# Opening loads written out, k products by rows, a shorter last product, and one product less per batch in a fused attention and MLP kernel

## The chip, the core and the metric

One core of a Trainium2 chip runs the whole program. The metric is the device time of one execution in microseconds (us). TensorE (PE) multiplies matrices and loads its weights in parallel (PEld); VectorE (DVE), ScalarE (ACT) and GpSimd (POOL) work elementwise; SyncE (SP) only issues DMA transfers here. Each engine takes its own instructions strictly in the order in which the program lists them.

## The reference, cut to what matters

```python
# attention: 4 batches, 8 heads, 576 positions, 64 wide; masks keep a window of 32 (4 heads) or 32 with stride 4
scores = where(mask, scale * q @ k.T, -1e9);  attn = softmax(scores);  x = attn @ v        # -> (4, 576, 512)
# first MLP, on x mixed with the x of the position before
xk = mu_k * x + (1 - mu_k) * x_prev;          xr = mu_r * x + (1 - mu_r) * x_prev
y  = sigmoid(xr @ w_r) * (relu(xk @ w_k)**2 @ w_v)          # w_r 512x512, w_k 512x1024, w_v 1024x512
# second MLP: mix over positions by a rank of 32, then over channels
u   = y + (y.T @ U @ V).T                                    # U 576x32, V 32x576
out = u + relu(u @ w_ch1) @ w_ch2                            # w_ch1 512x2048, w_ch2 2048x512
```

The weights come as 64-bit floats, read as two 32-bit words; the kernel turns them into 32-bit floats on the chip.

## The kernel before, in words

**Arithmetic.** A weight piece is 128x512. To convert one (`cv_bits`, lines 385 to 392) takes an `Abs` on ACT (L385) and four DVE operations (L386, L387, L389, L392). The first MLP's 20 pieces are `w1raw`: pieces 0 to 3 are w_r, 4 to 11 w_k, 12 to 19 w_v (`places`, line 1146). The first half batch (c = 0, 288 positions) multiplies whole 32-bit floats. For c = 1 to 7 each operand is cut into a high and a low part (`hi_lo`; in the rows `wh` and `wl`, L352 on ACT and L349 on DVE or POOL), and each product becomes three faster ones (L815 to L817). `split_weight` cuts the 20 pieces while c = 1 runs; meanwhile `cv_w2` converts the second MLP's 32 pieces (tile `w`, not `wx`) and writes them to a buffer in HBM, `w2f`.

**Stages.** Attention goes by units of one head pair and one part of a batch: the first four alone (`attend`), all later ones two at a time (`attend2`). A unit's chain crosses all engines: scores on PE (L597 or L676), mask and minimum on DVE (L537), exponentials on ACT (L546), sum and reciprocal on DVE (L551, L552), scaling on POOL (L557), transposes on PE (L628 or L714), a copy on ACT (`pts`, L352), the product with v on PE (L640 or L732), a copy to `x`. `mix` makes xk and xr of it: a difference `d` on POOL, then L769 on DVE. A half batch has 20 quanta (`quanta`): 4 tiles r, 8 tiles k, 8 (for c = 0, 16 half) tiles v. For c = 0 the r products go by rows (`r_row`, L828): as soon as piece p and mix p are there, four products into four PSUM banks `psM`. Its k tiles (L812) each need four pieces at once. Then come y @ U (`y_tr`, `u_mm`, L908 to L927), @ V (`v_mm`, `us`), and the second MLP in five groups (`ch1`, `ch2`), the last lines of which add and store the result.

**Order.** The code lists operations with durations; `plan` orders them per engine, by the longest way to the end, within a window of 160 operations, and keeps the best of 24 passes. Where it sees PE idle for over 600 ns it puts in products of zeros (`zero`, L1308). So a change of the list can move instructions anywhere.

**Lines touched.** The first loads stand at lines 1176 to 1183; `single`, `visit` and `fresh` bring in the attention units; `VISIT0`, `VISIT`, `CONV0`, `SPLIT` say at which quantum a visit, a conversion or a cut is listed. The rows of U past 576 are zeros, so in the last 64 positions of a batch `u_mm` multiplies half empty tiles, which L916 clears:

```python
            nc.tensor.matmul(acc(), lhsT=us[:n, t, :], rhs=hi()[:n], start=(t == 0), stop=False)
            nc.tensor.matmul(acc(), lhsT=us[:n, t, :], rhs=lo()[:n], start=False, stop=(t == NT - 1))
```

Of the kernel before, what the change touches and what calls it, by code (L numbers as in the profile page):

```python
# [62 lines left out]
SPLIT = (-4, -4, -3, -3, -1, -1, 0, 0, 1, 1, 2, 2, 5, 5, 6, 6, 7, 7, 8, 8)  # L63
# [15 lines left out]
def tile_attention_mix_channel(  # L79
# [708 lines left out]
    def quanta(c):  # L788
# [94 lines left out]
        q += [lambda o=o: k_tile(o) for o in range(8)]  # L883
# [18 lines left out]
    def y_tr(b, t, tag):  # L902
# [10 lines left out]
        sub("DVE", DM, lambda: lo()[:n], lambda: pt()[:n], lambda: f32(hi()[:n]), [(pt,), (hi,)], [(lo,)], psum=True)  # L913
        if n < P:
            for x in (hi, lo):
                op("POOL", 250, lambda x=x: nc.gpsimd.memset(f32(x()[n:]), 0.0), [], [(x, "rest")], 40)  # L916
        yhl[b, t] = (hi, lo, P)

    def u_mm(b, t, tag):
# [3 lines left out]
        hi, lo, n = yhl.pop((b, t))  # L923
# [5 lines left out]
        pe(2 * 233, run, [(hi,), (lo,), (hi, "rest"), (lo, "rest")] + [("us", g) for g in range(4)], [(acc,)], "f32r", 400)  # L929
# [168 lines left out]
    accs = {}  # L1098

    def ch2(g, j, hid):  # L1100
# [4 lines left out]
        for o in range(4):  # L1105
            acc = accs[g][o]

            def run(o=o, acc=acc):
                a = acc()[:, :n]
                for e in range(2):  # L1110
                    wh, wl = (t()[:, o * P : (o + 1) * P] for t in rows2_w[2 * j + e])
                    xh, xl = (t()[:, e * n : (e + 1) * n] for t in (hh, hl))
                    nc.tensor.matmul(a, lhsT=wh, rhs=xh, start=(j == 0 and e == 0), stop=False)  # L1113
                    nc.tensor.matmul(a, lhsT=wl, rhs=xh, start=False, stop=False)  # L1114
                    nc.tensor.matmul(a, lhsT=wh, rhs=xl, start=False, stop=(j == 7 and e == 1))  # L1115

            pe(6 * (MMW if g else MMQ), run, [(t,) for e in range(2) for t in rows2_w[2 * j + e]] + kh, [(acc,)], "f32r")
# [3 lines left out]
        for o in range(4):  # L1121
# [8 lines left out]
            step = Q if last and o == 3 else n  # L1130
            for c0 in range(0, n, step):
                c = slice(c0, c0 + step)
                dve(step, lambda acc=acc, ot=ot, u_=u_, c=c: nc.vector.tensor_tensor(
                    out=ot()[:, c], in0=acc()[:, c], in1=u_()[:, c], op=ALU.add),
                    [(acc,), ku], [(ot, c0) if last else (ot,)], two=True, psum=True)
                dma(P * step * 4, lambda o=o, ot=ot, c=c: nc.sync.dma_start(
# [35 lines left out]
    def next_piece():  # L1172
        src, k, _ = jobs[len(loaded)]
        loaded.append(cv_load(src, k))

    a_load(0, ["qk"])
    load(P * 4 * (P + NALL * KW), lambda: nc.sync.dma_start(cst_t, cst), ("cst",))
    next_piece()
    a_load(0, ["v"])
    load(P * 32, lambda: nc.sync.dma_start(mu_t, mu), ("mu",))  # L1180
    a_load(1, ["qk"])
    next_piece()
    a_load(1, ["v"])
# [47 lines left out]
    for c in range(NCH - 1):  # L1231
        cur = quanta(c) if c else first
        for n in range(NQ):
            if c == 0:
# [168 lines left out]
```

## Time and profile before

| what | value |
|---|---|
| median of 3 runs | 758.99 us (758.56 to 760.91) |
| profiled execution, its own time | 759.92 us |
| its span, first to last instruction | 758.1 us |
| PE busy | 739.3 us, 98% |
| DVE, ACT, POOL busy | 567.9, 393.1, 388.3 us |
| mean granted clock of TensorE | 0.997 |

The profiled execution is 0.93 us above the median of the runs; 1.8 us of it lie outside the span. Busy PE includes the products of zeros, so it is not useful work alone.

### The profile page before, as it was taken

The page shows a single profiled execution, that of the slowest core. Times are in us where ns is not written, and L with a number is a line of the kernel's source. Part 1 is how long each engine was busy: PE and PEld are TensorE (multiplying, and loading weights), DVE is VectorE, ACT ScalarE, POOL GpSimd, SP SyncE. Part 2 cuts the span into 40 slices and gives each one's busy share as a digit, 9 for nine tenths or more (in the row PEclk, how much of TensorE's full clock was granted, in tenths as well). Part 3 has the DMA queues.
Part 4 walks back from the last instruction along what each step waited for, and adds up shares of the span by engine and source line. Part 5 has one row for each costly group of instructions (what it writes and reads, how often), then busy time and mean ns, then how long its engine had stood idle before and what let it go on. Part 6 is the DMA issues. An engine that isn't in the chain of part 4 may idle for free.

```text
span 758.1 us, 18341 instructions
## 1 busy us (share of the span) xinstructions
PE 739.3 (98%) x6921; PEld 677.6 (89%) x6921; DVE 567.9 (75%) x1335; ACT 393.1 (52%) x995; POOL 388.3 (51%) x408
## 2 busy tenths in 40 slices
PE   8899999999999999999999999999999999999997
PEld 6667999999999999999999998888988989898986
DVE  5999989999898845775677778675888765575632
ACT  4578795767585746372555454343453434343310
POOL 1331464646464635273765677544677554456500
PEclk9999999999999999999999999999999999999999
DMA  9767346776756540557543252132532212042001
GB/s 333 238 255 246 133 148 192 267 248 202 267 179 205 176 157 1 196 160 225 178 153 100 94 181 100 57 125 83 171 102 84 85 56 84 29 140 70 15 1 55
DMA packets 53223, 109.77 MB, mean 145 GB/s; under 512 B 5648, under 2 KB 15888, under 8 KB 53136
## 3 DMA queue, kind: packets, MB, share of 16 engines
q1 hardware_dynamic: 53136, 108.62, 43.4%
q8 instruction: 54, 0.88, 0.5%
q14 instruction: 33, 0.27, 0.1%
HBM read 86.05 MB, written 22.54 MB: 143 GB/s over the span
## 4 chain that ended last, share of the span: by engine, by line
PE 83%; DVE 7%; POOL 3%; issue 3%; DMA 3%; ACT 1%; SPq 0%; DVEq 0%; POOLq 0%; ACTq 0%
PE psM L815 10%; PE psM L816 9%; PE psM L817 9%; PE psS L1115 8%; PE psS L1113 8%; PE psS L1114 8%; PE psM L1036 7%; PE psM L1037 6%; PE psM L1038 6%; PE psM L812 4%; PE psS L732 2%; PE psS L676 1%; DMA uf<-us 1%; POOL cl L347 1%; DVE ok L1073 1%
## 5 line engine op out<-in xcount | busy, mean ns | idle before, releaser
L347 POOL TENSOR_TENSOR cl<-sums,ch 128x512 fp32r<-128x512 f32 x72 | 98.6, 1369 | 93.5 <-ACT ch L352 62.4
L1113 PE MATMUL psS<-hh,rh 128*128 128x512 f32 (+1 forms) x320 | 119.3, 373 | 1.8 <-DVE us L949 1.5
L1115 PE MATMUL psS<-hl,rh 128*128 128x512 f32 (+1 forms) x320 | 119.4, 373 | 0.4 <-DVE hl L1051 0.3
L1114 PE MATMUL psS<-hh,rl 128*128 128x512 f32 (+1 forms) x320 | 118.9, 372 | 0.0
L352 ACT ACTIVATE ch<-sums 128x512 fp32r<-128x512 f32 (+1 forms) x104 | 57.5, 562 | 104.7 <-DVE sums L472 97.0
L815 PE MATMUL psM<-xk,wh 128*128 128x288 f32 x336 | 101.7, 303 | 0.0
L816 PE MATMUL psM<-xk,wl 128*128 128x288 f32 x336 | 99.5, 296 | 0.0
L817 PE MATMUL psM<-xk,wh 128*128 128x288 f32 x336 | 99.3, 295 | 0.0
L347 POOL TENSOR_TENSOR cl<-st,ch 128x256 fp32r<-128x256 f32 x80 | 66.9, 852 | 50.9 <-PE psM L1038 34.7
L472 DVE TENSOR_TENSOR sums<-st 128x256 f32<-128x256 f32 (+1 forms) x144 | 86.2, 646 | 7.8 <-POOL cl L347 3.9
L347 POOL TENSOR_TENSOR xk<-m,xk 128x288 fp32r<-128x288 f32 x56 | 54.8, 992 | 36.2 <-ACT xk L352 18.8
L1115 PEld LDWEIGHTS psS<-hl,rh 128*128 128x128 f32 x320 | 60.3, 188 | 12.3 <-DVE hl L1093 1.0
L1113 PEld LDWEIGHTS psS<-hh,rh 128*128 128x128 f32 x320 | 60.3, 188 | 11.7 <-DVE us L949 1.7
L1114 PEld LDWEIGHTS psS<-hh,rl 128*128 128x128 f32 x320 | 60.3, 188 | 9.4
L815 PE MATMUL psM<-k2s,wh 128*128 128x288 f32 x224 | 67.2, 300 | 0.0
L816 PE MATMUL psM<-k2s,wl 128*128 128x288 f32 x224 | 66.1, 295 | 0.2 <-issue 0.2
L817 PE MATMUL psM<-k2s,wh 128*128 128x288 f32 x224 | 66.0, 295 | 0.0
L815 PEld LDWEIGHTS psM<-xk,wh 128*128 128x128 f32 x336 | 63.5, 189 | 0.7 <-DVE wl L349 0.2
L347 POOL TENSOR_TENSOR k2s<-k,k2s 128x288 fp32r<-128x288 f32 x49 | 45.1, 926 | 36.7 <-ACT k2s L352 34.2
L816 PEld LDWEIGHTS psM<-xk,wl 128*128 128x128 f32 x336 | 63.7, 190 | 0.1
L817 PEld LDWEIGHTS psM<-xk,wh 128*128 128x128 f32 x336 | 63.7, 190 | 0.0
L1093 DVE SCALAR_TENSOR_TENSOR hl<-ort,hh 128x512 fp32r<-128x512 f32 x32 | 26.0, 811 | 46.3 <-ACT hh L1092 46.2
(152 smaller groups left out, 2137.1 us busy)
## 6 DMA issues: line engine op xcount, KB each, us to landing
st<-w2f SPq DMA_DIRECT2D x96, 256.0 KB, 3.1
w<-w2raw SPq DMA_DIRECT2D x32, 512.0 KB, 5.1
w<-w1raw SPq DMA_DIRECT2D x20, 512.0 KB, 5.7
w2f<-w SPq DMA_DIRECT2D x32, 256.0 KB, 2.6
raw<-qk SPq DMA_DIRECT2D x16, 320.0 KB, 6.4
ytmp<-y SPq DMA_DIRECT2D x32, 144.0 KB, 2.6
yb<-ytmp SPq DMA_DIRECT2D x4, 1152.0 KB, 6.8
uf<-us SPq DMA_DIRECT2D x32, 144.0 KB, 1.9
```

What stands on the lines that cost most here:

```text
L347: op("POOL", t, lambda: nc.gpsimd.tensor_tensor(out=out_(), in0=a(), in1=b(), op=ALU.subtract), r, w, 40, lock=True)
L352: act(n, lambda: nc.scalar.activation(out_(), in_(), AF.Copy), r, w, psum, strided)
L472: dve(k * Q, lambda: nc.vector.tensor_tensor(out=q(sm_, n, k)(), in0=a(), in1=b(), op=op_), [(s1,), (s2,)], [(sm_, key)], two=True)
L815: nc.tensor.matmul(a, lhsT=wh, rhs=xh, start=start, stop=False)
L816: nc.tensor.matmul(a, lhsT=wl, rhs=xh, start=False, stop=False)
L817: nc.tensor.matmul(a, lhsT=wh, rhs=xl, start=False, stop=stop)
L1036: nc.tensor.matmul(a, lhsT=wh()[:, wi], rhs=xh()[:, ci], start=(k == 0), stop=False)
L1037: nc.tensor.matmul(a, lhsT=wl()[:, wi], rhs=xh()[:, ci], start=False, stop=False)
L1038: nc.tensor.matmul(a, lhsT=wh()[:, wi], rhs=xl()[:, ci], start=False, stop=(k == len(parts) - 1))
L1113: nc.tensor.matmul(a, lhsT=wh, rhs=xh, start=(j == 0 and e == 0), stop=False)
L1114: nc.tensor.matmul(a, lhsT=wl, rhs=xh, start=False, stop=False)
L1115: nc.tensor.matmul(a, lhsT=wh, rhs=xl, start=False, stop=(j == 7 and e == 1))
```

## The change

1. The first loads follow a written order (`LOADS`, `begin`, `fetch`): the second unit's q and k come before the first unit's v; one piece is converted per step in the opening (`convert_to(t + 1, 1)`).
2. For c = 0 the first four k tiles go by rows (`k_row`), as the r tiles did.
3. The first two-unit step is a `visit` at quantum 0 instead of part of the last `single`; VISIT, MIX for c = 0 and one entry of SPLIT move.
4. `plan` takes the differences `d` 20 us earlier in its ranking, and puts in fewer and partly narrower products of zeros (35 of 512 and 17 of 224 columns for 55 of 512).
5. In a batch's last 64 positions the low part goes to rows 64 to 127 of the same tile, and U is repeated there: one product instead of two, and no clearing.
6. In the last `ch2`, tile 3 is multiplied in two parts of 384 and 128 columns; its adds and stores follow the parts.

```diff
+MIX0 = ((7, 0, "r"), (8, 1, "r"), (13, 0, "k"), (13, 2, "r"), (14, 1, "k"), (17, 2, "k"), (18, 3, "r"), (19, 3, "k"))
-VISIT0 = (4, 12)
-VISIT = (1, 10)
-CONV0 = [min(20, 7 + n) for n in range(20)]
+VISIT0 = (0, 4, 12)
+VISIT = (0, 11)
+CONV0 = 7
+LOADS = ("q0 c w q1 m", "q2 v0 v1 w", "q3 v2 w w", "w w w v3", "")
-SPLIT = (-4, -4, -3, -3, -1, -1, 0, 0, 1, 1, 2, 2, 5, 5, 6, 6, 7, 7, 8, 8)
+SPLIT = (-4, -4, -3, -3, -1, -1, 0, 0, 1, 1, 2, 4, 5, 5, 6, 6, 7, 7, 8, 8)
-FILL, FILL_FROM, FILL_NS = 0.7, 600.0, 0.453
+FILL, FILL_FROM, FILL_NS, FILL_COLD = 0.6, 600.0, 0.453, 7000.0
+EARLIER = {"d": -20}
...
-            return late
+            return [late[o.i] + 1000.0 * EARLIER.get(o.kind, 0) for o in ops]
...
-                    o.before = (x, wide, int(FILL * room / (FILL_NS * wide)))
+                    pace = FILL_NS * (2 if o.at < FILL_COLD else 1)
+                    o.before = (x, wide, int(FILL * room / (pace * wide)))
...
+        def k_row(p):
+
+            if p == 0:
+                kacc.update((o, bank("M")) for o in range(4))
+            for o in range(4):
+                pe(MM1, lambda o=o: nc.tensor.matmul(
+                    kacc[o]()[:, :HS], lhsT=whole_w[2 + p, 0]()[:, o * P : (o + 1) * P], rhs=cols(xk0, 4 + p),
+                    start=(p == 0), stop=(p == 3)), [(whole_w[2 + p, 0],), (xk0, 4 + p)], [(kacc[o],)], mode, spare=True)
+            if p == 3:
+                for o in range(4):
+                    k_out(o, kacc[o])
...
-        sub("DVE", DM, lambda: lo()[:n], lambda: pt()[:n], lambda: f32(hi()[:n]), [(pt,), (hi,)], [(lo,)], psum=True)
-        if n < P:
-            for x in (hi, lo):
-                op("POOL", 250, lambda x=x: nc.gpsimd.memset(f32(x()[n:]), 0.0), [], [(x, "rest")], 40)
-        yhl[b, t] = (hi, lo, P)
+        to, rows = (lo, slice(0, n)) if n == P else (hi, slice(n, P))
+        sub("DVE", DM, lambda: to()[rows], lambda: pt()[:n], lambda: f32(hi()[:n]), [(pt,), (hi,)], [(to, "lo")], psum=True)
+        yhl[b, t] = (hi, lo) if n == P else (hi,)
...
-            nc.tensor.matmul(acc(), lhsT=us[:n, t, :], rhs=hi()[:n], start=(t == 0), stop=False)
-            nc.tensor.matmul(acc(), lhsT=us[:n, t, :], rhs=lo()[:n], start=False, stop=(t == NT - 1))
+            for i, y in enumerate(parts):
+                nc.tensor.matmul(acc(), lhsT=us[:, t, :], rhs=y(), start=(t == 0 and i == 0), stop=(t == NT - 1))
...
+    ENDS = ((0, 3 * Q // 2), (3 * Q // 2, 2 * Q))
...
+        end = g == len(GROUPS) - 1 and j == 7
+        for o, (c0, c1) in [(o, c) for o in range(4) for c in (ENDS if end and o == 3 else ((0, n),))]:
...
-            step = Q if last and o == 3 else n
-            for c0 in range(0, n, step):
+            for c0, c1 in ENDS if last and o == 3 else ((0, n),):
...
-        for u in us_:
-            if u + 2 < NU:
-                a_load(u + 2)
+        for d in (0, 2):
+            for what in ("qk", "v"):
+                for u in us_ if d == 0 or nunit > NPAIR else ():
+                    fetch(u + d, what)
...
-        single(1 if t < NPAIR else 2)
-        convert_to(t + 1)
+        begin(LOADS[t])
+        single(1 if t < NPAIR else 0)
+        convert_to(t + 1, 1)
...
-    up[:S] = um
+    up[:S], up[S:] = um, um[S - NT * P :]
```

**Place one: the first transfers and the first conversion.** SP's first eleven issues before (`raw<-qk` and `raw<-v` are a unit's operands, `w_...` the pieces; line numbers of the two kernels differ):

```order
L526 DMA raw<-qk 128x640
L1177 DMA cst_t<-cst 128x448
L368 DMA w_100<-w1raw 128x512
L530 DMA raw<-v 128x640
L1180 DMA mu_t<-mu 128x8
L526 DMA raw<-qk 128x640
L368 DMA w_106<-w1raw 128x512
L530 DMA raw<-v 128x640
L526 DMA raw<-qk 128x640
L530 DMA raw<-v 128x640
L368 DMA w_143<-w1raw 128x512
```

The same of the change:

```order
L535 DMA raw<-qk 128x640
L1208 DMA cst_t<-cst 128x448
L377 DMA w_100<-w1raw 128x512
L535 DMA raw<-qk 128x640
L1210 DMA mu_t<-mu 128x8
L539 DMA raw<-v 128x640
L535 DMA raw<-qk 128x640
L539 DMA raw<-v 128x640
L377 DMA w_135<-w1raw 128x512
L535 DMA raw<-qk 128x640
L539 DMA raw<-v 128x640
```

The second unit's scores operand moved from the sixth place to the fourth, the second weight piece from the seventh to the ninth. DVE before, behind the first unit's minimum:

```order
L551 TENSOR_SCALAR sm<-sm 128x5
L552 RECIPROCAL sm<-sm 128x5
L386 TENSOR_SCALAR wx<-wx 128x512
L387 TENSOR_SCALAR wx<-wx 128x512
L537 ISA pr,mn<-psS,cst_t 128x64
```

DVE of the change, from the same place (the lines left out are the rest of the second unit's mask and minimum):

```order
L560 TENSOR_SCALAR sm<-sm 128x5
L561 RECIPROCAL sm<-sm 128x5
L546 ISA pr,mn<-psS,cst_t 128x64
...
L395 TENSOR_SCALAR wx<-wx 128x512
L396 TENSOR_SCALAR wx<-wx 128x512
L398 SCALAR_TENSOR_TENSOR wx<-w_100,wx 128x512
L401 SCALAR_TENSOR_TENSOR wx<-w_100,wx 128x512
```

The second unit now stands ahead of the first piece's conversion.

**Place two: PE around the k tiles of c = 0.** Before (L828 is `r_row`, L812 the k tiles):

```order
L1308 MATMUL psS<-zero 128x512 x11
L714 MATMUL psS<-cst_t,pr 128x128 x4
L828 MATMUL psM<-xk_301,wx 128x288 x4
L732 MATMUL psS<-pts,raw 64x32 x32
L676 MATMUL psS<-raw 32x64 x32
L828 MATMUL psM<-xk_301,wx 128x288 x4
L812 MATMUL psM<-xk_301,wx 128x288 x20
L714 MATMUL psS<-cst_t,pr 128x128 x4
```

PE of the change (L837 is `r_row`, L852 `k_row`, L821 the k tiles that stay):

```order
L837 MATMUL psM<-xk_325,wx 128x288 x4
L852 MATMUL psM<-xk_325,wx 128x288
L723 MATMUL psS<-cst_t,pr 128x128 x4
L852 MATMUL psM<-xk_325,wx 128x288 x2
L741 MATMUL psS<-pts,raw 64x32 x32
L685 MATMUL psS<-raw 32x64 x32
L852 MATMUL psM<-xk_325,wx 128x288 x13
L1340 MATMUL psM<-zero 128x512 x3
L821 MATMUL psM<-xk_325,wx 128x288 x16
```

The last r row now stands ahead of the first pair's transposes and products with v, and 16 k products stand around these.

**Place three: DVE at the k tiles of c = 1.** Before (`w_...` on the left are pieces of the second MLP, `k_...` the k tiles' results, `wl` the cut of the first MLP's pieces):

```order
L389 SCALAR_TENSOR_TENSOR w_1065<-w_1029,w_1065 128x512
L862 SCALAR_TENSOR_TENSOR k_1369<-psM,rt 128x288
L392 SCALAR_TENSOR_TENSOR w_1065<-w_1029,w_1065 128x512
L862 SCALAR_TENSOR_TENSOR k_1369<-psM,rt 128x288
L386 TENSOR_SCALAR w_1188<-w_1188 128x512
L349 TENSOR_TENSOR wl<-wx,wh 128x512
L862 SCALAR_TENSOR_TENSOR k_1369<-psM,rt 128x288
L387 TENSOR_SCALAR w_1188<-w_1188 128x512
L349 TENSOR_TENSOR wl<-wx,wh 128x512
L862 SCALAR_TENSOR_TENSOR k_1369<-psM,rt 128x288
```

The change at the same tiles:

```order
L886 SCALAR_TENSOR_TENSOR k_1367<-psM,rt 128x288
L358 TENSOR_TENSOR wl<-wx,wh 128x512
L886 SCALAR_TENSOR_TENSOR k_1367<-psM,rt 128x288
L358 TENSOR_TENSOR wl<-wx,wh 128x512
L395 TENSOR_SCALAR w_1051<-w_1051 128x512
L886 SCALAR_TENSOR_TENSOR k_1367<-psM,rt 128x288
L358 TENSOR_TENSOR wl<-wx,wh 128x512
L886 SCALAR_TENSOR_TENSOR k_1367<-psM,rt 128x288
```

Most of the second MLP's conversions now come after these tiles.

## Rows read from the trace of the kernel before

**Rows 1.** The page: busy us, share of the span, instructions of each engine.

```profile
PE 739.3 (98%) x6921; PEld 677.6 (89%) x6921; DVE 567.9 (75%) x1335; ACT 393.1 (52%) x995; POOL 388.3 (51%) x408
```

**Rows 2.** Busy time by stretch: length, then PE, PEld, DVE, ACT, POOL, clock, DMA.

```profile
5.00:24.65 19.65, 17.51 (x327) 12.87 (x325) 15.82 (x73) 11.05 (x45) 5.75 (x8) 1.00 0.90 324
24.65:72.40 47.75, 42.88 (x531) 32.82 (x528) 46.52 (x141) 34.14 (x101) 12.40 (x16) 1.00 0.75 253
82.73:107.74 25.01, 23.61 (x295) 23.12 (x294) 23.66 (x80) 19.78 (x68) 11.75 (x15) 0.93 0.49 156
107.74:300.00 192.26, 192.10 (x2631) 188.51 (x2630) 158.64 (x467) 128.94 (x375) 104.64 (x126) 1.00 0.57 189
300.00:400.00 100.00, 97.08 (x758) 94.75 (x757) 69.98 (x115) 48.30 (x97) 57.23 (x53) 1.00 0.54 174
```

**Rows 3.** Timeline of the opening, PE and DVE: start, us, engine, line, operation.

```profile
1.46 4.10 PE L1308 MATMUL psS<-zero 128*128 128x512 f32 x9 [1.46 <-DVE zero L1304]
5.49 0.66 PE L597 MATMUL psS<-raw 64*32 64x64 f32 x40
6.17 0.23 DVE L537 CUSTOM_DVE_ANT_0 pr<-psS,cst_t 128x64 f32<-128x64 f32 x1 [4.76 <-PE psS L597]
23.96 0.69 DVE L392 SCALAR_TENSOR_TENSOR wx<-w,wx 128x512 int32<-128x512 int32 x1
41.83 2.21 PE L828 MATMUL psM<-xk,wx 128*128 128x288 f32 x8
71.09 1.29 DVE L392 SCALAR_TENSOR_TENSOR wx<-w,wx 128x512 int32<-128x512 int32 x2
```

**Rows 4.** Timeline of PE after the k tiles of c = 1.

```profile
99.42 1.37 PE L732 MATMUL psS<-pts,raw 64*64 64x32 f32 x80 [1.40 <-ACT pts L352]
101.71 0.61 PE L815 MATMUL psM<-xk,wh 128*128 128x288 f32 x1
104.28 0.30 PE L816 MATMUL psM<-xk,wl 128*128 128x288 f32 x1
104.42 0.29 PE L817 MATMUL psM<-xk,wh 128*128 128x288 f32 x1
```

**Rows 5.** First transfers: SP's issues of cst and v; us to landing.

```profile
1.19 0.42 SPq L1177 DMA_DIRECT2D cst_t<-cst  x1
2.13 0.43 SPq L530 DMA_DIRECT2D raw<-v  x1
cst_t<-cst SPq DMA_DIRECT2D x1, 224.0 KB, 3.4
raw<-v SPq DMA_DIRECT2D x1, 320.0 KB, 5.9
```

**Rows 6.** DVE's groups from 5 to 72.4 us: busy us, mean ns.

```profile
L392 DVE SCALAR_TENSOR_TENSOR wx<-w,wx 128x512 int32<-128x512 int32 x20 | 15.6, 783 | 0.2
L769 DVE SCALAR_TENSOR_TENSOR m<-d,mu_t,x 128x288 f32<-128x288 f32 x3 | 1.5, 506 | 0.0
```

**Rows 7.** Busy time by stretch around that wait, columns as above.

```profile
102.00:104.00 2.00, 2.00 (x9) 2.00 (x9) 2.00 (x18) 2.00 (x7) 1.79 (x3) 0.50 0.76 236
```

**Rows 8.** Timeline of PE at y @ U.

```profile
299.67 0.40 PE L927 MATMUL psS<-yl,us 128*128 128x512 f32 x1
299.91 0.30 PE L815 MATMUL psM<-k2s,wh 128*128 128x288 f32 x1
304.14 0.50 PE L927 MATMUL psS<-yl,us 128*128 128x512 f32 x1 [0.65 <-POOL yl L916]
```

**Rows 9.** Timeline: products of 256 columns, the last product, the last adds.

```profile
735.28 0.28 PE L1037 MATMUL psM<-tA,ch 128*128 128x256 f32 x1
735.40 0.28 PE L1038 MATMUL psM<-tA,ch 128*128 128x256 f32 x1
753.52 0.39 PE L1115 MATMUL psS<-hl,rh 128*128 128x512 f32 x1
753.95 0.76 DVE L1133 TENSOR_TENSOR ot<-psS,ug 128x256 f32<-128x256 f32 x2 [0.70 <-PE psS L1115]
```

More of the change, by code (lines that the diff above doesn't have):

```diff
@@ L62 @@
 SIDE_AT = 9
-SPLIT = (-4, -4, -3, -3, -1, -1, 0, 0, 1, 1, 2, 2, 5, 5, 6, 6, 7, 7, 8, 8)
+AHEAD = 3
+PREP = (0, 5, 12)
+SPLIT = (-4, -4, -3, -3, -1, -1, 0, 0, 1, 1, 2, 4, 5, 5, 6, 6, 7, 7, 8, 8)
 SPLIT_ENG = ("DVE",)
@@ L134, in plan @@
             o.i, o.deps, o.tiles, o.done = i, set(), [], None
+            first = o.w[0][0]
+            o.kind = first.args[2] if isinstance(first, Lazy) else first
             for k in o.r:
@@ L882, in quanta @@
         q = [lambda o=o: (r_row if whole else r_tile)(o) for o in range(4)]
-        q += [lambda o=o: k_tile(o) for o in range(8)]
+        q += [lambda o=o: (k_row if whole and o < 4 else k_tile)(o) for o in range(8)]
         if whole:
@@ L922, in u_mm @@
         acc = uacc[b]
-        hi, lo, n = yhl.pop((b, t))
+        parts = yhl.pop((b, t))
         def run():
-            nc.tensor.matmul(acc(), lhsT=us[:n, t, :], rhs=hi()[:n], start=(t == 0), stop=False)
-            nc.tensor.matmul(acc(), lhsT=us[:n, t, :], rhs=lo()[:n], start=False, stop=(t == NT - 1))
-        pe(2 * 233, run, [(hi,), (lo,), (hi, "rest"), (lo, "rest")] + [("us", g) for g in range(4)], [(acc,)], "f32r", 400)
+            for i, y in enumerate(parts):
+                nc.tensor.matmul(acc(), lhsT=us[:, t, :], rhs=y(), start=(t == 0 and i == 0), stop=(t == NT - 1))
+        pe(len(parts) * 233, run, [(parts[0],), (parts[-1], "lo")] + [("us", g) for g in range(4)], [(acc,)], "f32r", 400)
         if t == NT - 1:
@@ L1104, in ch2, with run @@
             accs[g] = [bank("S") for _ in range(4)]
-        for o in range(4):
+        end = g == len(GROUPS) - 1 and j == 7
+        for o, (c0, c1) in [(o, c) for o in range(4) for c in (ENDS if end and o == 3 else ((0, n),))]:
             acc = accs[g][o]
-            def run(o=o, acc=acc):
-                a = acc()[:, :n]
+            def run(o=o, acc=acc, c0=c0, c1=c1):
+                a = acc()[:, c0:c1]
                 for e in range(2):
                     wh, wl = (t()[:, o * P : (o + 1) * P] for t in rows2_w[2 * j + e])
[L1112 to L1117, printed above, removed]
+                    xh, xl = (t()[:, e * n + c0 : e * n + c1] for t in (hh, hl))
+                    nc.tensor.matmul(a, lhsT=wh, rhs=xh, start=(j == 0 and e == 0), stop=False, skip_group_check=c0 > 0)
+                    nc.tensor.matmul(a, lhsT=wl, rhs=xh, start=False, stop=False, skip_group_check=c0 > 0)
+                    nc.tensor.matmul(a, lhsT=wh, rhs=xl, start=False, stop=(j == 7 and e == 1), skip_group_check=c0 > 0)
+            k_acc = [(acc, c0)] if end and o == 3 else [(acc, x) for x, _ in ENDS] if g == len(GROUPS) - 1 and o == 3 else [(acc,)]
+            pe(6 * (3 + 0.4487 * (c1 - c0)), run, [(t,) for e in range(2) for t in rows2_w[2 * j + e]] + kh, k_acc, "f32r")
         if j < 7:
@@ L1129, in ch2 @@
                 u_, ku = ot, (ot,)
[L1130 to L1133 removed]
+            for c0, c1 in ENDS if last and o == 3 else ((0, n),):
+                c = slice(c0, c1)
+                dve(c1 - c0, lambda acc=acc, ot=ot, u_=u_, c=c: nc.vector.tensor_tensor(
                     out=ot()[:, c], in0=acc()[:, c], in1=u_()[:, c], op=ALU.add),
[L1135 to L1136 removed]
+                    [(acc, c0) if last and o == 3 else (acc,), ku], [(ot, c0) if last else (ot,)], two=True, psum=True)
+                dma(P * (c1 - c0) * 4, lambda o=o, ot=ot, c=c: nc.sync.dma_start(
                     out[o, :, t0 + c.start : t0 + c.stop], ot()[:, c]), [(ot, c0) if last else (ot,)], [("out", g, o, c0)])
@@ L1160, in tile_attention_mix_channel, with convert_to @@
     converted = 0
-    AHEAD = 3
-    def convert_to(n):
+    def convert_to(n, ahead=None):
         nonlocal converted
         while converted < min(n, len(jobs)):
-            while len(loaded) < min(converted + AHEAD, len(jobs)):
+            while len(loaded) < min(converted + (ahead or AHEAD), len(jobs)):
                 src, k, _ = jobs[len(loaded)]
@@ L1170, in convert_to, with fetch, begin @@
             converted += 1
[L1172 to L1183, printed above, removed]
+    fetched = set()
+    def fetch(u, what):
+        if u < NU and (u, what) not in fetched:
+            fetched.add((u, what))
+            a_load(u, [what])
+    def begin(names):
+        for x in names.split():
+            if x == "w":
+                src, k, _ = jobs[len(loaded)]
+                loaded.append(cv_load(src, k))
+            elif x == "c":
+                load(P * 4 * (P + NALL * KW), lambda: nc.sync.dma_start(cst_t, cst), ("cst",))
+            elif x == "m":
+                load(P * 32, lambda: nc.sync.dma_start(mu_t, mu), ("mu",))
+            else:
+                fetch(int(x[1:]), {"q": "qk", "v": "v"}[x[0]])
     nunit = 0
@@ L1246, in tile_attention_mix_channel @@
                 divided += 1
-            for when, p, which in MIX:
+            for when, p, which in MIX0 if c == 0 else MIX:
                 if when == n + 1:
```

10 lines of the change are left out of this document (6 added, 4 removed).

## The prediction

> **What bounds the kernel now.** The page first: PE is busy 98% of the span [rows 1], so time can only go where PE waits, runs slowly or multiplies more than it must. The stretches come next. From 107.74 to 300 us PE is busy 192.10 of 192.26 us [rows 2]: there only fewer products help. Before that it is another picture. From 24.65 to 72.40 us DVE is busy 46.52 of 47.75 us while PE, its products of zeros included, has 42.88 [rows 2]; up to 24.65 us DVE has 15.82 of 19.65 us. The timeline says what DVE makes: the fourth weight piece is ready at 23.96 + 0.69 = 24.65 us, the twentieth at 71.09 + 1.29 = 72.38 us [rows 3]. The second half of the v products of c = 0 needs pieces 16 to 19, so these 16 products cannot begin before DVE has made the last. Up to about 72 us, then, the kernel is as fast as DVE's queue, and what PE does earlier in between is worth nothing by itself. From 82.73 to 107.74 us both are near full, DVE with 23.66 of 25.01 us [rows 2], and there PE has its one long wait: 1.40 us at 99.42 us for ACT's copy of `pts`, and behind it slow products [rows 4].
>
> **The opening (parts 1 to 4).** Three things move on DVE's queue.
>
> Its start. Nine products of zeros hold PE from 1.46 to 5.56 us, so the first scores run at 5.49 and DVE begins at 6.17, 0.68 us later [rows 3]. With four instead of nine they end by about 3.3 us; the masks land at 1.19 + 3.4 = 4.59 us [rows 5], and the scores' operand stands ahead of them on the queue. DVE can begin at about 5.0 us: 1.17 us earlier.
>
> The second unit. It now stands ahead of the first piece, so whatever delays it delays the whole queue. Its operand takes the place on the transfer queue where the first v stood, which landed at 2.13 + 5.9 = 8.03 us [rows 5]. Scores at about 8.25 put its DVE work at 8.25 + 0.68 = 8.9 us. DVE has nothing else between the first unit's reciprocal, at about 7.4, and then: 1.5 us idle, beside the 1.0 us that it waits for the exponentials. Before, DVE was busy 15.82 us between 5.00 and 24.65, thus idle 1.17 + 2.66. So the idle time behind the start is about the same, and the fourth piece is ready at 24.65 - 1.17 = 23.5 us. By the queue's list, what follows up to the twentieth piece is the same work with one mix of c = 1 more, 0.51 us [rows 6]. Term **a**: 0.51 - 1.17 = -0.7 us for the twentieth piece and all behind it. Bounds: if the pieces of the new order land late or the unit ahead stalls, the start's whole gain is lost and the mix paid, +0.5; if DVE also loses its stretching, -3.0 (see the third rival).
>
> The k rows. The last r row ran at 41.83 us [rows 3]. In the new order DVE has, between the fourth piece and the mix for that row, three and a half pieces at some 2.3 us, five mixes, a pair's minima (1.3) and a reciprocal (0.4): 23.5 + 8.0 + 2.5 + 1.7 = 35.7 us. The row's four products take 2 us, the 16 k products 7.8, the pair among them 2.5, and ACT must first free the banks: PE is through by about 49. Four more pieces, a pair's minima and three mixes bring DVE to piece 11 by about 51: PE waits 2.3 us, works through four k tiles, a pair and the first v half (7.8 + 2.5 + 7.8) to 69.1, and waits 2.6 for the twentieth piece. These 4.9 us of slack are where the k rows' gain goes: nothing in the sum.
>
> **c = 1.** The wait at 99.42 us is the end of a chain: `pts` stood on ACT behind a `rt` that waits for DVE to free a slot with its k operation, and DVE had seven operations on second-MLP pieces between its first cuts for c = 1 and the fifth k result, by the order. In the new order there are two, so five fewer at 0.4 to 0.8 us, and per k tile DVE has one k and one cut, about 1.1 us where PE needs 1.7 (12 products, 0.14 apart [rows 4]). In the 192 us behind, the same sequence of transposes, copy and products passes without such a wait [rows 2]. I take the wait as gone, -1.40. [...] Ten products take 104.28 - 101.71 = 2.57 us [rows 4] in place of 1.4: 1.2 us, and they go with the wait. Term **b**: -2.6 us. Bounds: 0 (another wait of the same kind) and -2.6.
>
> **One product less (part 5).** Four batches lose one product of 512 columns each, 299.91 - 299.67 = 0.24 us apiece [rows 8], in stretches where PE has no slack. Term **c**: -0.95 us, and only a stall could hide it. At 304.14 us one of these products waited 0.65 us for POOL's clearing of the tile [rows 8], which goes; now the product waits for DVE's subtraction into the same tile, as all others do. Term **d**: -0.65 (bounds -1.0 and 0).
>
> **The end (part 6).** Before, the last product ends at 753.52 + 0.39 = 753.91 us and the two adds at 754.71 [rows 9]. Now six products of 384 and six of 128 columns replace six of 512. Products of 256 columns stand 0.12 apart [rows 9], those of 512 0.24; 384 lies at 0.18, six make 1.08. For 128 the trace has no row: at least half of 0.12, at most 0.12, the shortest spacing seen with full weights. I take 0.12, the nearest row: 1.08 + 0.72 - 1.44 = +0.36 us for the last product. The add of 384 runs beside the last six; the add of 128, about 0.3 us, ends at 753.91 + 0.36 + 0.1 + 0.3 = 754.67. Term **e**: -0.1 (bounds -0.45 with 0.06 apart, and +0.2).
> [...]
>
> **Elsewhere.** The planner reorders stretches between 300 and 740 us as well, PE waiting 2.92 us from 300 to 400 [rows 2], 0.65 of them counted above. I leave the rest at 0, within 1.5 either way.
>
> **Sum:** -0.7 - 2.6 - 0.95 - 0.65 - 0.1 = -5.0 us. Against the profiled execution's own 759.92 that is 754.9; it lies 0.93 above the median of the runs, so the median becomes **754.0 us**.
>
> **Rivals.**
> *The wait in c = 1 comes back elsewhere.* The visits moved too, and the copy of `pts` still stands behind a `rt`, now of the seventh k tile. For it: DVE's and ACT's queues are as full as before. Against it: the five operations that left. Term b falls away: 754.0 + 2.6 = 756.6 us.
> *DVE is not as tight as I think.* In the opening L392 takes 783 ns on average [rows 6] and 0.69 at most other places [rows 3]; such stretches, 20 pieces times four operations, hold some 5 us, and they fall when POOL works at the same time. The earlier `d` could free 3 of them: 754.0 - 3 = 751.0 us. Against it: POOL's work is the same.
> *Slower: PE goes cold in the opening.* There are fewer and narrower products of zeros, and with small products alone the clock has been seen to fall [rows 7]. At half clock the 32 products of r and k rows, 0.49 each, would take 15.6 us more. PE has 4.9 us of slack, so from ten such products on they cost time, and beyond 12 us of extra (25 products: the slack, the 5.0 and the 2.3 of 0.3%) the kernel is slower than before. If all run so: 754.0 + 15.6 - 4.9 = 764.7 us. Against it: at the rows PE is continuously at work, and at 104.28 it had regained its pace after ten products [rows 4].
> [...]
>
> **How the numbers follow.** Forecast 0.50, the wait elsewhere 0.30, a looser DVE 0.12, cold 0.06, others 0.02. A measurement of this kernel tells about 0.3%, 2.3 us, from no change: below 756.7 counts as faster. The forecast with its bounds (a, d, e and elsewhere, 752.5 to 757) lies there nine times in ten, 0.45; the first rival, 755 to 758.5, about four in ten, 0.13; the looser DVE always, 0.12: faster 0.70. Slower is the cold opening and a little else, 0.07; the same is what remains, 0.23. The range from 751.0 to 758.5 us leaves out the cold opening, about half of the looser DVE and the end of the first rival, some 0.15.
>
> **What would show it.** DVE's first operation at about 5.0 us; the fourth piece at 23.5, the twentieth near 71.7; c = 1 on PE about 0.7 us earlier (counting the pair that now stands behind its first tiles); no wait of PE over 0.5 us and no clock under 1.0 between 80 and 110 us; 16 products y @ U fewer by four and no clearing on POOL; the last add 0.1 to 0.4 us nearer to the start of the last products. The prediction is wrong if the twentieth piece comes later than 72.4, if PE waits anew at a copy of `pts`, if the clock falls in the opening for longer than PE's slack, or if the reordered stretches past 300 us wait 2 us more.

## The result, and the profile after

The change takes 750.62 us (median of 4, 750.15 to 751.39) where the kernel before took 759.83 beside it: ratio 0.9885, 95% interval 0.9867 to 0.9902. It is 9.2 us faster by the medians, 8.7 by the ratio; the forecast was 5.0 us. 750.62 lies 0.4 us below the lower end of the forecast's range, 751.0. The profiled execution's own time is 750.69 us, its span 748.8.

The page, as [rows 1], and busy time by stretch, as [rows 2], with one stretch more:

```profile
PE 733.4 (98%) x6920; PEld 675.5 (90%) x6920; DVE 564.4 (75%) x1335; ACT 393.1 (53%) x995; POOL 381.5 (51%) x400
```

```profile
5.00:24.65 19.65, 17.07 (x282) 13.09 (x282) 14.77 (x71) 13.41 (x52) 5.78 (x9) 0.91 0.89 312
24.65:72.40 47.75, 43.44 (x538) 33.07 (x536) 46.27 (x141) 33.71 (x102) 12.22 (x17) 1.00 0.79 268
82.73:107.74 25.01, 23.11 (x436) 22.54 (x437) 22.96 (x72) 20.28 (x65) 13.78 (x16) 0.95 0.23 75
107.74:300.00 192.26, 191.67 (x2625) 188.15 (x2624) 156.41 (x477) 128.88 (x383) 100.61 (x123) 1.00 0.60 199
300.00:400.00 100.00, 100.00 (x808) 99.22 (x807) 72.16 (x128) 51.45 (x106) 57.13 (x55) 1.00 0.56 184
105.00:108.40 3.40, 3.40 (x78) 3.23 (x75) 3.22 (x21) 3.40 (x15) 2.52 (x3) 0.51 0.66 190
```

The opening and c = 1 are no fuller than before; in the first stretch the clock is 0.91, since it stood at half from 9.5 to 12.9 us. The change is from 300 to 400 us: PE is busy all 100.00 us with 808 products, where [rows 2] had 97.08 us and 758. The timeline of PE and DVE at the places of [rows 3], [rows 4] and [rows 9], and DVE at 356 us:

```profile
3.75 0.90 PE L606 MATMUL psS<-raw 64*32 64x64 f32 x40 [0.23 <-DMA raw<-qk]
8.67 0.66 PE L606 MATMUL psS<-raw 64*32 64x64 f32 x40 [2.46 <-DMA raw<-qk]
...
4.69 0.23 DVE L546 CUSTOM_DVE_ANT_0 pr<-psS,cst_t 128x64 f32<-128x64 f32 x1 [3.29 <-PE psS L606]
...
9.35 0.23 DVE L546 CUSTOM_DVE_ANT_0 pr<-psS,cst_t 128x64 f32<-128x64 f32 x1 [2.20 <-PE psS L606]
...
15.18 0.23 DVE L546 CUSTOM_DVE_ANT_0 pr<-psS,cst_t 128x64 f32<-128x64 f32 x1 [1.13 <-PE psS L606]
...
22.91 1.28 DVE L401 SCALAR_TENSOR_TENSOR wx<-w,wx 128x512 int32<-128x512 int32 x2
...
71.61 0.68 DVE L401 SCALAR_TENSOR_TENSOR wx<-w,wx 128x512 int32<-128x512 int32 x1
...
72.44 6.54 PE L821 MATMUL psM<-k,wx 128*128 128x288 f32 x26 [0.93 <-DVE wx L401]
...
103.65 1.37 PE L741 MATMUL psS<-pts,raw 64*64 64x32 f32 x80 [1.90 <-ACT pts L361]
...
106.42 0.44 PE L825 MATMUL psM<-k2s,wl 128*128 128x288 f32 x1
106.66 0.44 PE L826 MATMUL psM<-k2s,wh 128*128 128x288 f32 x1
...
356.75 1.29 DVE L1040 TENSOR_TENSOR tmp<-ug 128x512 f32<-128x512 f32 x2 [0.38 <-DMA ug<-uf]
357.96 0.45 DVE L971 TENSOR_TENSOR us<-psS,yb 128x288 f32<-128x288 f32 x1
...
744.15 0.34 PE L1139 MATMUL psS<-hl,rh 128*128 128x384 f32 x1
...
744.72 0.27 PE L1138 MATMUL psS<-hh,rl 128*128 128x128 f32 x1
...
744.83 0.28 PE L1139 MATMUL psS<-hl,rh 128*128 128x128 f32 x1
...
745.14 0.76 DVE L1157 TENSOR_TENSOR ot<-psS,ug 128x384 f32<-128x384 f32 x2 [0.96 <-PE psS L1139]
```

The fourth piece is ready at 24.19 us, the twentieth at 72.29 (before 24.65 and 72.38, forecast 23.5 and 71.7). In c = 1 PE waits again for the copy of `pts`, longer than in [rows 4], and again runs slowly behind it (clock 0.51 from 105.0 to 108.4 us). Who made PE wait from 107.74 us to the end, before (the six longest of nine) and then after (us in total, times, longest):

```profile
PE psS L1113 <- DVE us L949: 1.5, 1, 1.5
PE psM L944 <- DVE ok L1073: 0.8, 2, 0.4
PE psS L927 <- POOL yl L916: 0.7, 1, 0.7
PE psM L1036 <- DVE ok L1073: 0.3, 1, 0.3
PE psS L1115 <- DVE hl L1051: 0.3, 1, 0.3
PE psS L927 <- DVE yl L349: 0.2, 1, 0.2
```

```profile
PE psS L685 <- issue: 0.6, 1, 0.6
PE psS L1137 <- ACT hh L1114: 0.4, 2, 0.2
PE psM L966 <- DVE ok L1095: 0.2, 1, 0.2
```

**Where the time went.** To compare kernels whose orders differ, I counted each PE product of the trace at its usual spacing (288 columns 0.1325 us, whole floats 0.2425, 512 columns 0.2325, 256 0.117, 384 0.173, 128 0.109, a score 0.013, a product with v 0.0163, zeros nothing). A transpose is entered with 0.07, too little: in fours they start 0.109 apart in both traces, and with 0.109 the bold column would be 2.2 us lower before and 2.3 in the change, the difference still -8.3. Lost time is the time at which so much useful work is done, minus that work. The columns below are cut at equal useful work (60, 80, 260, 520 and 690 us of it); the times in the head are those of the kernel before. The losses are those of one profiled execution each, which lies up to 2.5 us from the median beside it.

| lost, us | to 90.5 | to 113.7 | to 299.2 | to 571.1 | to 743.5 | median, us |
|---|---|---|---|---|---|---|
| before | 30.5 | 3.2 | 5.4 | **11.9** | 2.4 | 759.8 |
| change | 29.5 | 3.7 | 5.8 | **3.6** | 2.7 | 750.6 |
| one_product | 34.1 | 0.4 | 8.4 | **4.5** | 2.4 | 755.1 |
| one_product_shifted | 32.3 | 0.4 | 7.2 | **4.3** | 2.4 | 751.7 |
| change_shifted | 34.7 | 0.4 | 8.0 | **3.4** | 2.7 | 756.6 |
| change_realigned | 30.7 | 2.3 | 6.2 | **5.0** | 2.7 | 751.9 |
| change_realigned_warm | 29.5 | 2.3 | 6.5 | **3.8** | 2.7 | 750.6 |
| change_k_tiles | 30.9 | 0.4 | 13.4 | **3.7** | 2.7 | 756.4 |
| one_product_old_order | 31.8 | 3.4 | 5.5 | 9.6 | 2.4 | 755.8 |
| two_products | 30.6 | 0.5 | 7.6 | 9.6 | 2.7 | 759.2 |
| opening_alone | 32.6 | 0.4 | 6.3 | 8.8 | 2.7 | 757.0 |
| replan_slack | 30.1 | 0.4 | 7.6 | 8.2 | 2.3 | 757.5 |
| replan_rate | 29.9 | 2.4 | 8.8 | 8.2 | 2.7 | 758.5 |
| no_clearing | 31.8 | 0.4 | 16.0 | 9.1 | 2.7 | 763.8 |

Change against before, from the unrounded losses: -1.1, +0.5, +0.4, -8.3, +0.3 us. With four products fewer (-0.93), the six products in two parts (+0.30) and 0.44 us less between the last product and the span's end, that is -9.2. The time came from 299 to 571 us, a stretch for which the forecast had no term but the 0.65 us of the clearing (and the four products, counted apart here). In no profile does the clock fall or a wait named "issue" (see below) of over 0.4 us lie in the bold column; both occur in the first three, which makes these less sure.

### The profile page after: what moved, and what is told of

Its sections match the earlier page's. It is cut to its first block, busy times and chain, and to the rows that moved or that the text cites. A ratio compares the mean times of both kernels' runs of the same rounds, so it can differ in the third digit from the quotient of the medians.

```text
span 748.8 us, 18318 instructions
## 1 busy us (share of the span) xinstructions
PE 733.4 (98%) x6920; PEld 675.5 (90%) x6920; DVE 564.4 (75%) x1335; ACT 393.1 (53%) x995; POOL 381.5 (51%) x400
## 4 chain that ended last, share of the span: by engine, by line
PE 88%; DVE 5%; DMA 3%; ACT 2%; issue 1%; SPq 0%; POOL 0%; DVEq 0%; ACTq 0%; POOLq 0%
PE psM L824 10%; PE psM L826 10%; PE psM L825 10%; PE psS L1139 9%; PE psS L1137 9%; PE psS L1138 9%; PE psM L1058 8%; PE psM L1060 8%; PE psM L1059 8%; PE psS L741 2%; DMA w<-w1raw 2%; PE psM L821 1%; PE psS L685 1%; DVE wx L401 1%; DVE wx L398 1%; DMA raw<-qk 1%
## 5 line engine op out<-in xcount | busy, mean ns | idle before, releaser
L1137 PE MATMUL psS<-hh,rh 128*128 128x512 f32 (+2 forms) x322 | 119.5, 371 | 0.4 <-ACT hh L1114 0.4
L1139 PE MATMUL psS<-hl,rh 128*128 128x512 f32 (+2 forms) x322 | 119.6, 371 | 0.0
L1138 PE MATMUL psS<-hh,rl 128*128 128x512 f32 (+2 forms) x322 | 119.2, 370 | 0.0
L824 PE MATMUL psM<-xk,wh 128*128 128x288 f32 x336 | 100.9, 300 | 0.0
L356 POOL TENSOR_TENSOR xk<-m,xk 128x288 fp32r<-128x288 f32 x56 | 52.4, 946 | 41.2 <-ACT xk L361 33.9
L1095 DVE TENSOR_TENSOR ok<-ok,psM 128x256 f32<-128x256 f32 (+1 forms) x96 | 46.4, 504 | 22.4 <-PE psM L1060 20.0
L356 POOL TENSOR_TENSOR k2s<-k,k2s 128x288 fp32r<-128x288 f32 x49 | 43.0, 879 | 35.0 <-ACT k2s L361 32.5
```

The source lines that it names most:

```text
L356: op("POOL", t, lambda: nc.gpsimd.tensor_tensor(out=out_(), in0=a(), in1=b(), op=ALU.subtract), r, w, 40, lock=True)
L824: nc.tensor.matmul(a, lhsT=wh, rhs=xh, start=start, stop=False)
```

## The experiments

Theories: **A**, part 5 leads the planner to another order of 300 to 520 us, and that order has no waits; **B**, part 5 is worth its products and their waits, and the rest comes from other parts; **C** came up on the way: PE waits where its instructions arrive in blocks. The median of the kernel before was 758.7 us beside the first four runs, 758.8 beside the shifted and replanned ones, 759.3 beside the last four. Differences in us are differences of ratios times 759 us, those to the change by its 0.9885.

**one_product**: part 5's lines in the kernel before.

```diff
-            nc.tensor.matmul(acc(), lhsT=us[:n, t, :], rhs=hi()[:n], start=(t == 0), stop=False)
-            nc.tensor.matmul(acc(), lhsT=us[:n, t, :], rhs=lo()[:n], start=False, stop=(t == NT - 1))
+            for i, y in enumerate(parts):
+                nc.tensor.matmul(acc(), lhsT=us[:, t, :], rhs=y(), start=(t == 0 and i == 0), stop=(t == NT - 1))
```

> The kernel before with part 5 alone (low part in rows 64 to 127, one product instead of two, no clearing). Theory A (the gain of the change lies in the order that the planner finds for 300 to 520 us once part 5 shortens its list; the waits there go): 6 to 9 us faster than before, PE's waits of 300 to 540 us fall from 4.2 us to under 1.5 us, and the opening and c = 1 stay as before. Theory B (part 5 is worth its four products and the waits at them, as forecast, and the rest of the gain came from other parts): 1.6 us faster, 1.0 to 2.2.

Ratio 0.9958 (0.9941 to 0.9975), -3.2 us. Neither as expected: the bold column falls by 7.4 us as A says, but 3.6 and 2.9 us are lost anew in the first and third (2.8 come back in the second). Part of that is a wait that the profile names "issue", inside bursts of score products; PE of this kernel:

```profile
141.44 0.99 PE L676 MATMUL psS<-raw 64*32 64x64 f32 x75
144.79 0.31 PE L676 MATMUL psS<-raw 64*32 64x64 f32 x5 [2.37 <-issue]
```

**one_product_old_order**: the planner sees the list of before; only what is issued differs.

```diff
-                op("POOL", 250, lambda x=x: nc.gpsimd.memset(f32(x()[n:]), 0.0), [], [(x, "rest")], 40)
+                op("POOL", 250, lambda: None, [], [(x, "rest")], 40)
...
+            for i, y in enumerate((hi, lo) if t < NT - 1 else (hi,)):
```

> Part 5's work in the order of the kernel before: the planner still sees two products and the clearing, but the clearing is left out and one product runs. Every other instruction stands where it stood. If the gain is the work that part 5 saves: the same as part 5 with a new order. Theory A (the order makes it): only the four products (0.95) and the wait for the clearing (0.65) go, 1 to 2.2 us faster than before, and the waits at 363 us (1.5 us for us) and those for ok stay.

Ratio 0.9966 (0.9950 to 0.9982), -2.6 us, slightly above the 1 to 2.2 us of A. The order is that of before, less the clearings and four products, and 9.6 us are lost in the bold column; with the order that the planner makes for the same work, 4.5. So of the 7.4 us that part 5 takes there, 2.3 come with its work alone and 5.1 with the new order. As whole kernels the two are hardly apart (0.9966 and 0.9958): part 5 alone loses 2.2 us more ahead of that column, and this kernel's profile lies 1.9 us above its median.

**two_products**: the change without part 5.

```diff
-        to, rows = (lo, slice(0, n)) if n == P else (hi, slice(n, P))
...
+                op("POOL", 250, lambda x=x: nc.gpsimd.memset(f32(x()[n:]), 0.0), [], [(x, "rest")], 40)
+        yhl[b, t] = (hi, lo)
```

> The changed kernel without part 5 (two products and the clearing, as before). Theory A: 5 to 9 us slower than the changed kernel, so 1 to 4 us faster than before, with PE waiting 2 us or more between 300 and 540 us. Theory B: 1.6 us slower than the changed kernel, so about 7.5 us faster than before.

Ratio 1.0014 (0.9999 to 1.0029): no faster than before and 9.8 us behind the change, beyond even A's 5 to 9. Without part 5 the other parts bring nothing in this measurement; 1.9 us of its loss is an "issue" wait at 228.5 us.

**opening_alone**: before with parts 1 and 2, part 3 without VISIT and SPLIT, and the fill of zeros.

```diff
+LOADS = ("q0 c w q1 m", "q2 v0 v1 w", "q3 v2 w w", "w w w v3", "")
+        q += [lambda o=o: (k_row if whole and o < 4 else k_tile)(o) for o in range(8)]
```

> The kernel before with the written loads, the k rows, the first pair by visit and the smaller fill of zeros alone; parts 5 and 6, the earlier d, VISIT and SPLIT as before. By the forecast's terms a and b: 2 to 3.3 us faster. By the trace of the changed kernel (PE starts 1.7 us earlier but has only 0.5 us left of it after c = 1): 0 to 1 us faster, within what a measurement tells from no change, unless the planner's order past 300 us comes out otherwise.

Ratio 0.9972 (0.9958 to 0.9986), -2.1 us, at the lower end of the forecast's terms, but not where these put it. In its trace the opening itself loses 2.1 us more than before, the wait in c = 1 goes (-2.8), and 3.1 us come from the bold column, by another order.

**replan_slack** and **replan_rate**: the same work in other orders.

```diff
-SLACK = 100.0
+SLACK = 110.0
```

```diff
-RATE = 285.0
+RATE = 280.0
```

> The kernel before with one number of the planner changed (its tolerance for an engine other than PE, 100 to 110 ns): the same work in another order. Theory A (the order of 300 to 520 us decides, and an edit draws a new one): the time moves by more than 1 us in either direction, and the waits of PE between 300 and 540 us change (4.2 us before). Rival (the order matters little, part 5's smaller load on DVE and POOL removes the waits): the same time within 1 us, with the waits at 303, 363 and 396 us about as before.

> The kernel before with the planner's transfer rate changed from 285 to 280: the same work in another order. As for the other order of the same work: theory A, the waits between 300 and 540 us change by over 1 us and the time with them, either way; rival, the same time within 1 us and the same waits.

Ratios 0.9986 (0.9968 to 1.0004) and 0.9997 (0.9984 to 1.0010): not told from before. The bold column fell to 8.2 us in both, so an edit does draw a new order, but neither draw comes near 4. In both, "issue" waits that are new cost 2.6 and 3.0 us.

**no_clearing**: both products over 64 rows, no clearing.

```diff
-        yhl[b, t] = (hi, lo, P)
+        yhl[b, t] = (hi, lo, n)
```

> The kernel before with both products of a batch's last 64 positions kept, but over 64 rows only, so that nothing needs clearing; the planner makes a new order. It splits part 5. If the gain of 300 to 520 us comes from the clearing's leaving the planner's list: PE loses there 4 to 5 us against its useful work (before 11.9, part 5 alone 4.5), and the kernel is 3 to 7 us faster. If it takes the whole of part 5 (one product and one tile of the ring of three less): 8 to 12 us are lost there as with the other orders of the same work, and it is 0 to 2 us faster.

Ratio 1.0053 (1.0028 to 1.0077), slower, which neither answer expected; the third column holds it (16.0 us). Of these, 6.7 are two "issue" waits and some 4 the half clock behind them (142.5 to 149.3 and 166.4 to 169.8 us), so the time is no price of the missing clearing. The bold column, 9.1 us, says that the clearing alone is not what the planner needs.

**one_product_shifted** and **change_shifted**: instructions put in front, the order kept.

```diff
+            if many and not shifted:
+                shifted, many = True, 7
+                for _ in range(50):
+                    nc.tensor.matmul(onto()[:32, :32], lhsT=zero[:, :32], rhs=zero[:, :32], start=True, stop=True)
```

> Part 5 alone in the kernel before, with the first nine products of zeros replaced by seven and by 50 tiny ones (32 x 32), so that every later PE instruction stands 96 places further back; the order is the same. In the trace of part 5 alone PE waits 1.73, 2.58 and 0.70 us inside bursts of score products, for nothing that the profile names, each time at an instruction whose number is 193 past a multiple of 256. Theory C (PE's instructions arrive in blocks of 256, and a burst that uses up a block in under 2.5 us waits for the next): the three waits go, 3 to 5 us faster than part 5 alone, 750 to 752 us when the kernel before takes 758.7. Rival (the waits belong to the score products or to memory traffic at that time): they stay, and the time is that of part 5 alone within 1 us.

> The changed kernel with the first four products of zeros replaced by two and by 42 tiny ones, so that every later PE instruction stands 80 places further back; the order is the same. Counted in the trace of the changed kernel, five blocks of 256 PE instructions would then be used up in about 1.7 us. Theory C: waits of 0.7 to 2.5 us appear at several of them, 1.5 to 5 us slower than the changed kernel (752 to 756 us). Rival: no new waits, same time within 1 us.

Ratios 0.9916 (0.9899 to 0.9933) and 0.9961 (0.9942 to 0.9980). Theory C both times: the three waits of part 5 alone are gone and it is 3.2 us faster; in the change four new ones appear and it is 5.8 us slower, a little beyond the 1.5 to 5 expected. One of them, PE of change_shifted:

```profile
60.13 1.02 PE L685 MATMUL psS<-raw 64*32 64x64 f32 x78
64.41 0.30 PE L685 MATMUL psS<-raw 64*32 64x64 f32 x2 [3.26 <-issue]
```

**change_realigned** and **change_realigned_warm**: another prefix; with zeros in front of the waiting products besides.

```diff
+        fills = [(2, 27), (1, 27), (1, 26)]
...
+            if hasattr(o, "mode_after"):
+                joins += 1
+                if joins == 9:
+                    onto, wide, many = o.first[0], CW, 7
```

> The changed kernel with the first three fills of zeros (4, 3 and 3 products of 512 columns) replaced by 2, 1 and 1 and by 27, 27 and 26 tiny ones, so that every later PE instruction stands 148 places further back; the order is the same. Counted in the trace of the changed kernel, only one block of 256 PE instructions is then used up in under 2.5 us (2.3), against three before and five in the kernel shifted by 80. Theory C (waits at block boundaries): no faster than the changed kernel by more than 1 us, 749.5 to 750.6, and 5 us faster than the one shifted by 80. Rival (any such prefix costs the opening): 752 us or more, as when shifted by 80.

> The same with seven products of zeros (512 columns, 1.6 us) put in front of the first pair's products with v in c = 1, where PE waited 1.90 us for the copy of pts and ran at half clock behind it; the prefix is 14 instructions shorter, so that all behind that place stands as in the realigned kernel. If the slow products after the wait come from PE's idle time before it (term b's second part, 1.2 us): the wait stays, the clock stays at full speed, 1 to 1.7 us faster than the realigned kernel. Rival (the small attention products alone let the clock fall, or the clock falls by chance): same time within 1 us.

Ratios 0.9892 (0.9866 to 0.9917) and 0.9879 (0.9852 to 0.9906): no "issue" wait is left, and the same time as the change (0.9885). So a prefix does not cost by itself. On the clock they tell nothing: in both profiles the clock stays full in c = 1, in the first behind the same wait. No version beat the change measurably.

**change_k_tiles**: the change without the k rows.

```diff
-        q += [lambda o=o: (k_row if whole and o < 4 else k_tile)(o) for o in range(8)]
+        q += [lambda o=o: k_tile(o) for o in range(8)]
```

> The changed kernel with all eight k tiles of c = 0 by tiles, as before. The forecast: the k rows' gain is lost in PE's slack before c = 1, so the same time within 1 us apart from waits at block boundaries, and c = 1 starts within 0.5 us of 79.3. Rival: the k rows carry the opening's gain, c = 1 starts 1.5 us later or more and the kernel is slower by as much. Past 320 us the order is that of the changed kernel, so the loss there stays at 3 to 4 us.

Ratio 0.9969 (0.9942 to 0.9995), 6.4 us behind the change. Where c = 1 starts (at 83.23 us; the pair now stands ahead of it) it has lost 1.6 us more than the change, 1.2 of them in an "issue" wait at 41.8 us. The rest is lost between 113 and 300 us (13.4 against 5.8): 3.8 us in two more such waits where the change has one of 0.8, 2.9 in two waits of its other order, and 1.7 at half clock (from 163.1 us). For the k rows themselves 0.4 us of the 1.6 is left.

## Why the prediction was right in its direction and half as large as the result

**What bounds the kernel: right as far as it went.** To 72.4 us DVE is still busy 46.27 of 47.75 us, and from 107.74 to 300 us PE 191.67 of 192.26. But the end of the opening was misread: in the kernel before, PE did not wait for the twentieth piece. Its v products (two rows of the trace each) run on through 72.4 us without a gap:

```profile
64.25 11.80 PE L812 MATMUL psM<-k,wx 128*128 128x288 f32 x48
```

The first product that needs the twentieth piece, the 20th of these, starts at 73.47 us, 1.1 after the piece was ready. In the change PE comes to it sooner, waits 0.93 us and starts it at 72.44.

**Term a (-0.7): near in size (-1.1 in the profile of the change), by luck.** The term was the twentieth piece's, and that came only 0.09 us earlier. DVE started at 4.69 us, 0.3 before the forecast's 5.0, but waited 2.20 us for the second unit's scores (forecast 1.5; they ran at 8.67, not 8.25) and 1.13 us for the third's, which the forecast does not have, so the fourth piece was 0.7 us late against it. The gain is PE's, which has done more before it comes to that piece. It is not firm: against before, other kernels with this opening lost 1.0 us less (change_realigned_warm), the same (two_products), 0.2 more (change_realigned), 2.1 more (opening_alone) and 4.2 more (change_shifted) at 60 us of useful work. In opening_alone the clock was at half from 26.9 to 33.7 us, in change_shifted there are "issue" waits.

**The k rows (nothing): right,** as far as one pair of profiles shows (0.4 us).

**Term b (-2.6): wrong; the first rival came true.** The wait for `pts` came back with 1.90 us at 103.65 us: +0.5 us instead of -2.6. The step that failed is "I take the wait as gone": I had counted DVE's operations between cuts and k results, but did not follow ACT's queue to the copy. ACT in the change, between the end of the transposes at 100.18 us and the copy:

```profile
100.17 0.62 ACT L361 ACTIVATE wh<-wx 128x512 fp32r<-128x512 f32 x1
100.70 0.39 ACT L881 ACTIVATE rt<-psM 128x288 f32<-128x288 f32 x1
101.69 0.44 ACT L361 ACTIVATE k2s<-k 128x288 fp32r<-128x288 f32 x1 [0.59 <-DVE k L886]
102.03 0.39 ACT L881 ACTIVATE rt<-psM 128x288 f32<-128x288 f32 x1
102.33 0.62 ACT L361 ACTIVATE wh<-wx 128x512 fp32r<-128x512 f32 x1
102.84 0.76 ACT L361 ACTIVATE pts<-psS 128x512 f32<-128x512 f32 x2
```

DVE's `k` holds ACT up for only 0.59 us; the rest of the 2.7 us is ACT's own work that stands ahead of the copy, two cuts `wh` among it. In change_shifted, where the transposes come 5.2 us later, the copy starts 3.2 us later and the wait is gone (0.4 us lost); in change_realigned both come 1.2 us later and PE waits as long (1.87 us). Of the price, the slow clock is some 1.4 us (3.7 lost in the change, 2.3 with the same wait at full clock in change_realigned); what decides whether the clock falls there stays open, and that the slow products go with the wait was my estimate.

**Term c (-0.95): right, -0.93. Term d (-0.65): right;** no kernel with part 5 waits there.

**Term e (-0.1; its own times give -0.04): wrong in its last step, +0.3.** The spacings were nearly as taken (0.17 us for 384 columns, 0.11 for 128, 744.72 to 744.83, together +0.30 against +0.36; the trace before did have 128 columns with full weights, the transposes L714, 0.109 apart from 55.72 to 56.04 us, so 0.12 was not the shortest spacing in it), but the add of 384 did not run beside the last six products: it starts at 745.14, behind the last one, because in the program only the last of the twelve products signals DVE. The 0.44 us less at the end is not part 6's: one_product, without it, has 3.69 us from the last product to the span's end, the change 3.70, before 4.14.

**"Elsewhere 0, within 1.5": the step that failed in size.** It was -8.3 us with term d in it. Shown is that part 5 with the planner's new order does most of it: seven kernels planned with it lose 3.4 to 5.0 us there, six planned without it 8.2 to 11.9, and part 5's work in the old order 9.6. The seven are not seven draws: past 320 us five have the change's order and two that of one_product. One place shows how. DVE before at 360 us, and the PE product that waits for it:

```profile
362.02 1.29 DVE L1018 TENSOR_TENSOR tmp<-ug 128x512 f32<-128x512 f32 x2 [3.69 <-DMA ug<-uf]
364.62 0.46 DVE L949 TENSOR_TENSOR us<-psS,yb 128x288 f32<-128x288 f32 x1 [1.30 <-DMA uf<-us]
...
365.13 0.39 PE L1113 MATMUL psS<-hh,rh 128*128 128x256 f32 x1 [1.53 <-DVE us L949]
```

`us` stands behind `tmp` on DVE, which waits 3.69 us for a transfer, and PE waits for `us`. After the change DVE has the same three operations in the same order, but hardly waits for the transfer (0.38 us): it was issued at 351.02 us, 5.4 us before DVE came to it, and took 5.7, where before it was issued at 354.86, 3.5 us ahead, and took 7.1. PE does not wait there. The named waits from 295 to 525 us fall from 4.0 to 0.2 us. With what they cost at their edges, the gaps of over 0.06 us beyond the usual spacing sum to 9.5 us in the bold column before and 2.2 after; closer spacing (below) gives 1.1 more. Why the planner finds this order only with all of part 5 (one product and one tile less, no clearing) is open; without the clearing alone it did not.

The forecast did not weigh where PE's blocks of instructions end. In the change it cost 0.8 us, in its shifted copy over 7 us of waits.

**The other rivals.** A looser DVE was to end at 751.0 us, near the measured time, but for a reason that did not come: DVE's four conversion operations took 48.6 us up to 72.4 where they had taken 49.7, so 1.1 us and not 3 were freed there, and the gain lies past 299 us. The stretching beside POOL is in the trace before: up to 72.4 us L392 took 954 ns on average where POOL was busy for over half of it (5 of 20) and 686 where POOL was idle (13); in the change the same operation took 782 (4) and 681 (14). The clock did fall in the opening, from 9.5 to 12.9 us, ahead of the r and k rows, and 3.4 us at half speed cost less than the slack of 4.9 that the forecast gave PE.

## What to carry to other kernels

An edit in a list that a planner orders has two prices, its work and the new order; hold the order fixed once (as one_product_old_order does) and read the order past the edit, not only at it. Compare kernels by the time at which equal useful work is done: it shows in one table where a gain arises and where it is spent. Before judging a change of under 1% in a kernel with bursts of tiny products, time it with a few dummy instructions in front, since their place alone moved this one by 6 us.

## What the runs showed of the hardware that was not expected

**Blocks of instructions.** The page of the change has this queue:

```profile
q8 instruction: 54, 0.88, 0.5%
```

54 packets of 16 KB for 13,840 products and weight loads are 256 for each. In the 14 traces PE waits 20 times over 0.4 us for "issue", 0.7 to 4.2 us from start to start, and each time the next PE instruction's number, counted with those that only wait, is 193 past a multiple of 256. The packet of a block starts within about 5 us of PE's beginning the block before it, sooner or later (3.9 us sooner to 5.0 later in the kernel before, 3.9 and 4.3 in the change), and the 20 waits end 2.2 to 2.8 us after their packet's start. In the change the block that was used up in 1.71 us (to 230.63) had the next one's packet start 1.27 us ahead of its own beginning, and PE did not wait; at the wait of 0.59 us (213.45) the packet started 0.09 us behind that beginning.

**Spacing.** Products of 256 columns stand 0.113 us apart for long stretches in the change (360 to 380 us) and 0.118 in the kernel before there (0.114 from 340 to 360 us), with the same operands. No run explains it.

**The clock.** The half clock (0.50 of full, for 3.41 us each time in the kernel before at 100.9 and in the change at 9.5 and 105.0 us) comes at other places from profile to profile, and in five of the fourteen not before the kernel's end: in the opening, or behind a long wait (105.0 us in the change, 65.7 in change_shifted, 142.5 in no_clearing). Of part 5 alone, twelve runs of one program took 751.5 to 758.0 us at mean granted clocks of 0.993 to 1.000; the fastest had 1.000, the slowest 0.998, so the clock is only part of the scatter.
